# Token-permuted column blocks, and the first z cast, turned and scored block by block, in an attention and MoE kernel

## The chip, the cores and the metric

The kernel runs on one core of one Trainium2 chip. The metric is device microseconds of one execution; "before" takes 1245.67 us (median of 5 runs, 1244.64 to 1246.48). A ratio between two kernels is the mean time of one kernel's fast runs over the mean of the other's fast runs of the same rounds, so it is not quite the ratio of the quoted medians. Names: TensorE is PE in the profile, its weight loads PEld, VectorE is DVE, ScalarE is ACT, GpSimd is POOL, SyncE is SP. A "q" behind a name (ACTq, SPq) is the engine's own queue at work on instructions such as the issue of a DMA.

## The reference

```python
# u, v: (8, 3008, 256), z: (8, 3008, 64), w_in: (256, 2048), w_out: (2048, 256)
scores = (1 / S) * z @ z.T                      # per batch, S = 3008
attn   = maximum(scores, 0) ** 2
x      = u * (attn @ v)                         # gated attention
h      = x.reshape(24064, 256) @ w_in
out    = (h * cos(h)) @ w_out
```

## The kernel before

A batch has 3008 rows: 6 column blocks of 512 (the last has 448), each 4 tiles of 128. For column block c and row block R, TensorE makes four score matmuls, ScalarE and VectorE apply relu and square, and TensorE multiplies with v into two accumulators. The MoE part of earlier tokens is woven in between. Score squares of later blocks (tt) come from DMA transposes of earlier ones. In batch 0 there is nothing earlier to weave in, so its first blocks wait for the loads. The parts that matter here:

```python
def rows(src, b, g):                     # 8 tiles of 128 rows: row j*128 + p on partition p
    r0 = g * G * P
    n = min(G, (S - r0) // P)
    full = src[b, r0:r0 + n * P, :].rearrange("(j p) d -> p j d", p=P)
    rest = src[b, r0 + n * P:S, :] if n < G else None
    return n, full, rest

def hold(dma):                           # a load waits until TensorE has come this far
    after(dma.ins, gate[0] if gate else before[-1], SYNC)
...
def first_z_load(g):                     # 3 groups: 8 loads in all, on SP's and ACT's queues
    ...
    nc.sync.dma_start(zf[:, 0:n // 2, :], full[:, 0:n // 2, :])
    nc.scalar.dma_start(zf[:, n // 2:n, :], full[:, n // 2:n, :])
    if rest is not None:
        nc.scalar.dma_start(zf[0:JLAST, n, :], rest)
        nc.sync.dma_start(zf[JLAST:P, n, :], rest)

def first_z_turn(g):                     # cast on VectorE, 8 transposes on TensorE, copy out
    nc.vector.tensor_copy(zst[:, j0 + 1:j0 + 1 + G, :], zfs[g])
    ...
    (nc.scalar.copy if g < 2 else nc.vector.tensor_copy)(zT[0][:, ...], tp[:, ...])   # shortened
...
# the order of work: an event's first number is its place in time; one column block is 8 long
scores.append((c * U + 4 * i / 3 - 3.1, [(b, c, R, 0), (b, c, R, 1)]))
at((-30, -2.5, 0.8)[g], 0, lambda g=g: first_z_turn(g))
first = [load_v(0, 0), load_u(0, 0), load_v(0, 1), load_v(0, 2), load_u(0, 1)]        # shortened
at(t + c * U + (1 if b or c not in (1, 2) else -3 * c), 0, lambda b=b, c=c: turn_u(b, c))
...
# a store: 256 rows, one DMA on ScalarE's queue
nc.scalar.dma_start(out[r0:r0 + 256, :].rearrange("(ts p) d -> p ts d", p=P), obs[m][:, 0:2, :])  # shortened
```

In PSUM the kernel keeps six rotating score banks and two accumulators.

Of the kernel before, what the change touches and what calls it, by code (L numbers as in the profile page):

```python
# [9 lines left out]
FP16 = mybir.dt.float16  # L10
FP32 = mybir.dt.float32
# [3 lines left out]
def kernel(  # L15
# [44 lines left out]
    ust = [kpool.tile([P, NDH, K, P], FP16, name=f"ust{i}") for i in range(2)]  # L60
# [32 lines left out]
    def rows(src, b, g):  # L93

        r0 = g * G * P
        n = min(G, (S - r0) // P)
        full = src[b, r0:r0 + n * P, :].rearrange("(j p) d -> p j d", p=P)
        rest = src[b, r0 + n * P:S, :] if n < G else None
        return n, full, rest

    def load_z(b):
        for g in range(NG):
            n, full, rest = rows(z, b, g)
            j0 = g * G + 1
            load(zst[:, j0:j0 + n, :], full)
            if rest is not None:
                for p0 in (0, JLAST):
                    load(zst[p0:p0 + JLAST, j0 + n, :], rest)
# [8 lines left out]
    def load_v(b, g):  # L117
        t = vs(b, g)
        n, full, rest = rows(v, b, g)
        load(t[:, 0:n, :], full)  # L120
        if rest is not None:
            for p0 in (0, JLAST):
                load(t[p0:p0 + JLAST, n, :], rest)
# [12 lines left out]
    def load_u(b, c):  # L136
        r0 = c * CW
        n = min(K, (S - r0) // P)
        st = ust[c % 2]
        for dh in range(NDH):  # L140
            ds = slice(dh * P, (dh + 1) * P)
            load(
                st[:, dh, 0:n, :],
                u[b, r0:r0 + n * P, ds].rearrange("(j p) d -> p j d", p=P))
            if n < K:
                load(st[0:JLAST, dh, n, :], u[b, r0 + n * P:S, ds])

    def turn_u(b, c):
        ut = utpool.tile([P, NDH, CW], FP16, name="ut")
        hold(nc.sync.dma_start_transpose(  # L150
            ut.rearrange("p h (j w) -> p (h j) w", w=P),
            ust[c % 2].rearrange("p h j w -> p (h j w)")))
        uts[(b, c)] = ut
# [17 lines left out]
    def first_z_load(g):  # L171
        zfs[g] = xpool.tile([P, NDH, TW], FP16, name="x")
        zf = zfs[g].rearrange("p h w -> p (h w)").bitcast(FP32).rearrange(
            "p (j d) -> p j d", d=dqk)
        zfs[g] = zf
        n, full, rest = rows(z, 0, g)
        nc.sync.dma_start(zf[:, 0:n // 2, :], full[:, 0:n // 2, :])
        nc.scalar.dma_start(zf[:, n // 2:n, :], full[:, n // 2:n, :])
        if rest is not None:
            nc.scalar.dma_start(zf[0:JLAST, n, :], rest)  # L180
            nc.sync.dma_start(zf[JLAST:P, n, :], rest)

    def first_z_turn(g):
        j0 = g * G
        last = g == NG - 1
        nc.vector.tensor_copy(zst[:, j0 + 1:j0 + 1 + G, :], zfs[g])  # L186
        for k, n in ((0, G), (G, 1))[0:1 + last]:
            tp = ps_w.tile([P, CW], FP32, name="w").bitcast(FP16).rearrange(
                "p (j w) -> p j w", w=P)
            for i in range(n):  # L190
                chain(nc.tensor.transpose(  # L191
                    tp[:, i, :],
                    zst[:, j0 + k + i:j0 + k + i + 2, :].rearrange("p j d -> p (j d)"),
                    ident))
            if g < 2:
                nc.scalar.copy(zT[0][:, j0 + k:j0 + k + n, :], tp[:, 0:n, :])  # L196
            else:
                nc.vector.tensor_copy(zT[0][:, j0 + k:j0 + k + n, :], tp[:, 0:n, :])
# [12 lines left out]
    def s_matmuls(b, c, R, p):  # L211
# [5 lines left out]
        for k in ((0, 1), (3, 2) if diagonal else (2, 3))[p]:  # L217
            s0 = k if diagonal else 0
            lo = 1 if k in ((1, 2) if diagonal else (1, 3)) else 0
            h = slice(lo * dqk, (lo + 1) * dqk)  # L220
# [69 lines left out]
    def av_chunks(b, c, sizes):  # L290
# [26 lines left out]
        def finish():  # L317
# [4 lines left out]
            while o < w:  # L322
                m, at = (t0 + o) // TW, (t0 + o) % TW
                n = min(w - o, TW - at)
                if m not in xs:
                    xs[m] = xpool.tile([P, NDH, TW], FP16, name="x")
                parts.append((xs[m][:, :, at:at + n], o, n))
                o += n
            for nh in range(NDH):
                for x, o, n in parts:  # L330
                    nc.vector.tensor_tensor(  # L331
                        x[:, nh, :], acc[nh][:, o:o + n], ut[:, nh, o:o + n], ALU.mult)
# [24 lines left out]
    def y_quantum(m, ts, f4):  # L357
# [6 lines left out]
        if f4 == NFT // FG - 1:  # L364
# [5 lines left out]
            i0 = i if m == NT - 1 else 0  # L370
            if i or m == NT - 1:
                r0 = m * TW + (ts - i + i0) * P
                nc.scalar.dma_start(
                    out[r0:r0 + (i + 1 - i0) * P, :].rearrange("(ts p) d -> p ts d", p=P),
                    obs[m][:, i0:i + 1, :])
# [17 lines left out]
    for b in range(B):  # L393
# [6 lines left out]
        for c in range(NC):  # L400
            if direct(b, c, c):
                for i in range(NC):
                    R = (c + i) % NC
                    scores.append((c * U + 4 * i / 3 - 3.1, [(b, c, R, 0), (b, c, R, 1)]))
# [32 lines left out]
    for b in range(B):  # L437
        t = b * span
        if b == 0:
            for g in range(NG):  # L440
                at(-100 + g, 0, lambda g=g: first_z_load(g))
                at((-30, -2.5, 0.8)[g], 0, lambda g=g: first_z_turn(g))
# [70 lines left out]
```

## Time and profile before

| | before |
|---|---|
| median | 1245.67 us |
| span of the profiled run | 1244.6 us |
| TensorE busy | 1234.4 us, 99% |
| first scores / first value matmul | 7.3 / 11.7 us |
| stall at 40 us | 2.63 us |
| stores | 96 |

The head of the page of before gives the span, and busy time, share of the span and instruction count of each engine:

```profile
span 1244.6 us, 20404 instructions
...
PE 1234.4 (99%) x7533; PEld 680.0 (55%) x7533; DVE 782.0 (63%) x1389; ACT 844.7 (68%) x1609; POOL 145.8 (12%) x201
```

The table by stretches of before: per stretch its length, then the busy time of PE, PEld, DVE, ACT and POOL with instruction counts, the granted clock, the DMA share and GB/s.

```profile
0.00:16.00 16.00, 12.96 (x65) 4.97 (x65) 10.26 (x22) 9.15 (x16) 7.72 (x15) 1.00 1.18 162
16.00:40.00 24.00, 24.00 (x126) 8.33 (x124) 21.27 (x34) 15.72 (x30) 4.29 (x6) 1.00 1.34 148
40.00:43.00 3.00, 0.37 (x5) 0.18 (x2) 0.83 (x2) 1.57 (x3) 0.36 (x1) 1.00 1.22 212
...
50.00:64.00 14.00, 12.67 (x61) 4.90 (x58) 10.97 (x18) 12.28 (x24) 6.14 (x8) 1.00 1.61 151
...
80.00:1240.00 1160.00, 1160.00 (x7151) 649.95 (x7150) 722.10 (x1287) 791.39 (x1511) 123.91 (x167) 1.00 0.71 114
```

From 80 to 1240 us TensorE never stands still, so a change can gain only before and after that. The timeline of before (start, duration, engine, line, what, count; in brackets the idle time before it and who ended it) shows the opening and the stall:

```profile
4.33 0.78 DVE L186 CAST zst<-x 128x512 f16<-128x512 f32 x1 [2.93 <-DMA x<-in_z_dram]
...
6.24 1.01 ACT L196 COPY zT_63<-w 128x1024 f16<-128x1024 f16 x1 [3.46 <-PE w L191]
...
7.30 1.03 PE L223 MATMUL w<-zT_63 64*128 64x512 f16 x4 [1.10 <-ACT zT_63 L196]
...
11.70 1.47 PE L310 MATMUL acc<-a,v_65 128*128 128x512 f16 x6
...
42.17 1.29 DVE L331 TENSOR_TENSOR x<-acc,ut 128x512 f16<-128x512 f32 x2 [2.46 <-DMA ut<-ust_62]
...
42.91 1.46 PE L310 MATMUL acc<-a,v_66 128*128 128x512 f16 x6 [2.63 <-DVE x L331]
```

and the chain of work that ended last (start, duration, what) leads the stall back to a DMA transpose of u:

```profile
31.03 11.05 DMA ut<-ust_62
```

### The profile page before, as it was taken

What the parts mean: (1) busy time and instruction counts of PE and PEld (TensorE: products, weight loads), DVE (VectorE), ACT (ScalarE), POOL (GpSimd) and SP (SyncE); (2) the same over time, 40 slices, a digit from 0 to 9 for tenths busy, and PEclk for the clock granted to TensorE, in tenths of its full rate; (3) what the DMA queues carried; (4) which work ended last, traced back from release to release, by engine and by line L of the source; (5) the groups of instructions that cost most, each with busy time, mean ns of one, the idle gap of its engine ahead of it and who ended that gap; (6) DMA issues with size and microseconds to landing.
All of it is one profiled execution on the core that took longest, in us unless ns stands there. A gap on an engine that the chain in (4) does not pass through costs nothing.

```text
span 1244.6 us, 20404 instructions
## 1 busy us (share of the span) xinstructions
PE 1234.4 (99%) x7533; PEld 680.0 (55%) x7533; DVE 782.0 (63%) x1389; ACT 844.7 (68%) x1609; POOL 145.8 (12%) x201
## 2 busy tenths in 40 slices
PE   9899999999999999999999999999999999999998
PEld 3355555555555555555555555555555555555556
DVE  7766666666666666656666566665666656666555
ACT  6666676666676766667766667766667766667646
POOL 3210101001010010100101011011010111100000
PEclk9999999999999999999999999999999999999999
DMA  9997958679576795757958569685695957957311
GB/s 162 152 174 129 141 91 119 114 122 142 99 117 111 117 144 106 115 111 110 149 101 121 107 109 150 101 129 99 109 158 92 129 101 112 152 101 108 72 33 45
DMA packets 484212, 144.85 MB, mean 116 GB/s; under 512 B 432400, under 2 KB 484112, under 8 KB 484112
## 3 DMA queue, kind: packets, MB, share of 16 engines
q1 hardware_dynamic: 356448, 88.73, 43.1%
q0 software_dynamic: 100400, 29.77, 24.7%
q10 hardware_dynamic: 27264, 25.06, 6.3%
q8 instruction: 59, 0.97, 0.3%
q14 instruction: 41, 0.34, 0.1%
HBM read 60.29 MB, written 24.64 MB: 68 GB/s over the span
## 4 chain that ended last, share of the span: by engine, by line
PE 97%; DMA 2%; DVE 0%; ACT 0%; issue 0%; DVEq 0%; ACTq 0%
PE acc L310 37%; PE w L361 26%; PE w L344 26%; PE w L223 6%; DMA tt<-a 1%; DMA ut<-ust_62 1%; PE acc L285 1%; DMA x<-in_z_dram 0%; DVE g L351 0%; PE w L191 0%; DVE x L331 0%; ACT zT_63 L196 0%; ACT rt L256 0%; DVE a L258 0%; DVE zst L186 0%
## 5 line engine op out<-in xcount | busy, mean ns | idle before, releaser
L361 PE MATMUL w<-w_out_71,g 128*128 128x256 f16 x3008 | 448.6, 273 | 0.0
L344 PE MATMUL w<-x,w_in_70 128*128 128x512 f16 x1504 | 445.6, 379 | 0.8 <-DVE g L351 0.8
L361 PEld LDWEIGHTS <-g 128*128 128x128 f16 x3008 | 294.2, 98 | 191.6 <-issue 1.4
L256 ACT ACTIVATE rt<-w 128x512 f16<-128x512 f32 x489 | 253.1, 613 | 121.2 <-PE w L223 121.2
L258 DVE TENSOR_TENSOR a<-rt 128x1024 f16<-128x1024 f16 x254 | 173.8, 691 | 180.8 <-ACT rt L256 178.3
L344 PEld LDWEIGHTS <-w_in_70 128*128 128x128 f16 x1504 | 147.0, 98 | 59.2 <-issue 3.9
L90 POOL DMA_DIRECT2D ust_62<-in_u_dram x64 | 44.7, 704 | 385.8 <-PE acc L310 355.9
L240 ACT ACTIVATE rt<-w 128x512 f16<-128x512 f32 (+3 forms) x176 | 62.8, 449 | 39.7 <-PE w L223 39.7
L331 DVE TENSOR_TENSOR x<-acc,ut 128x64 f16<-128x64 f32 (+7 forms) x178 | 69.6, 431 | 29.1 <-PE acc L310 26.6
L310 PE MATMUL acc<-a,v_65 128*128 128x512 f16 x336 | 85.8, 380 | 0.0
L310 PEld LDWEIGHTS <-v_66 128*128 128x128 f16 x552 | 51.9, 98 | 61.8 <-issue 14.1
L310 PEld LDWEIGHTS <-v_65 128*128 128x128 f16 x552 | 51.6, 98 | 60.0 <-issue 13.1
L310 PEld LDWEIGHTS <-v_67 128*128 128x128 f16 x552 | 51.9, 98 | 58.7 <-issue 11.1
L310 PEld LDWEIGHTS <-v_68 128*128 128x128 f16 x552 | 51.9, 98 | 57.7 <-issue 10.9
L310 PE MATMUL acc<-a,v_66 128*128 128x512 f16 x312 | 79.4, 379 | 2.6 <-DVE x L331 2.6
L310 PE MATMUL acc<-a,v_68 128*128 128x512 f16 x312 | 79.2, 379 | 0.0
L310 PE MATMUL acc<-a,v_67 128*128 128x512 f16 x312 | 79.1, 379 | 0.0
L368 ACT ACTIVATE ob<-w 128x256 f32<-128x256 f32 x188 | 73.0, 388 | 5.3 <-PE w L361 5.3
L241 DVE TENSOR_TENSOR a<-rt 128x512 f16<-128x512 f16 (+3 forms) x176 | 47.3, 321 | 44.0 <-ACT rt L240 44.0
L90 POOL DMA_DIRECT2D ust_61<-in_u_dram x48 | 36.5, 766 | 224.4 <-PE acc L310 206.7
L310 PE MATMUL acc<-tt,v_68 128*128 128x512 f16 (+1 forms) x240 | 62.2, 371 | 0.0
L310 PE MATMUL acc<-tt,v_67 128*128 128x512 f16 (+1 forms) x240 | 62.1, 371 | 0.0
(1546 smaller groups left out, 1399.8 us busy)
## 6 DMA issues: line engine op xcount, KB each, us to landing
out_dram<-ob ACTq DMA_DIRECT2D x92, 256.0 KB, 2.3
ust_61<-in_u_dram POOLq DMA_DIRECT2D x48, 128.0 KB, 4.0
ust_62<-in_u_dram POOLq DMA_DIRECT2D x32, 128.0 KB, 4.4
a<-a SPq DMA_TRANSPOSE x132, 3.0
v_65<-in_v_dram POOLq DMA_DIRECT2D x4, 512.0 KB, 6.1
v_66<-in_v_dram POOLq DMA_DIRECT2D x4, 512.0 KB, 6.6
v_68<-in_v_dram POOLq DMA_DIRECT2D x4, 512.0 KB, 6.2
v_67<-in_v_dram POOLq DMA_DIRECT2D x4, 512.0 KB, 6.2
```

The source lines that it names most:

```text
L90: hold(nc.gpsimd.dma_start(dst, src))
L223: chain(nc.tensor.matmul(sp[:, s0 * P:], zt[h, R * K + k + 1 - lo, :], zt[h, j0 + s0:j0 + K, :].rearrange("p j w -> p (j w)"), start=True, ...
L240: nc.scalar.activation(rt[:, i, k * P:], banks[k][:, k * P:], AF.Relu)
L241: nc.vector.tensor_tensor(t[:, k, k:, :].rearrange("p s w -> p (s w)"), rt[:, i, k * P:], rt[:, i, k * P:], ALU.mult)
L256: nc.scalar.activation(rt[:, i, :], banks[k], AF.Relu)
L258: nc.vector.tensor_tensor(t.rearrange("p s k w -> p k s w")[:, 2 * p:2 * p + 2], rv, rv, ALU.mult)
L285: chain(nc.tensor.matmul(accs[(b, c)][nh], vs(b, NG - 1)[h, G - 1, nh * P:(nh + 1) * P], a[h], start=False, stop=False))
L310: chain(nc.tensor.matmul(acc[nh][:, 0:wn], vs(b, j // G)[:, j % G, nh * P:(nh + 1) * P], a, start=(n == 0), stop=(n == NJ - 2)))
L331: nc.vector.tensor_tensor(x[:, nh, :], acc[nh][:, o:o + n], ut[:, nh, o:o + n], ALU.mult)
L344: chain(nc.tensor.matmul(hp, w_in16[:, k, ft * P:(ft + 1) * P], x[:, k, :], start=(k == 0), stop=(k == NDH - 1)))
L361: chain(nc.tensor.matmul(ys[m][:, 0:D], gs[(m, f4)][:, ft % FG, ts * P:(ts + 1) * P], w_out16[:, ft, :], start=(ft == 0), stop=(ft == NFT ...
L368: nc.scalar.activation(obs[m][:, i, :], ys[m][:, 0:D], AF.Copy, bias=0.0, scale=inv_s2)
```

## The change

Rows of a column block are dealt out so that partition p holds rows 4p to 4p + 3 of the block. Each partition's piece of z, v, u and out is then contiguous in DRAM: 1 KB instead of 256 B for z, 4 KB instead of 1 KB for v, 4 KB instead of 512 B for u. The first z is loaded, cast, turned and scored per column block instead of per group of 8 tiles, so that the first scores need only a sixth of z. u of block 1 is loaded and turned earlier. The price: output tiles of 512 tokens and column blocks are shifted against each other by 64 rows per batch, so a store often has to be cut into 64-partition pieces. Cut to its core:

```diff
-        full = src[b, r0:r0 + n * P, :].rearrange("(j p) d -> p j d", p=P)
+        full = src[b, r0:r0 + n * P, :].rearrange("(p k) d -> p k d", k=n)
 ...
+    def first_z_load(c):                 # 6 blocks x 2 halves + 2 for the rest: 14 loads
 ...
+        for p0, eng in ((0, nc.sync), (JLAST, nc.scalar)):
+            h = slice(p0, p0 + JLAST)
+            eng.dma_start(zfs[c // 2][h, k0:k0 + n, :], full[h])
+            if rest is not None:
+                eng.dma_start(zfs[c // 2][h, k0 + n, :], rest)
 ...
-                    scores.append((c * U + 4 * i / 3 - 3.1, [(b, c, R, 0), (b, c, R, 1)]))
+                    t = c * U + 4 * i / 3 - 3.1 if c else (-3.1, -1.8, 0.6, 1.9, 3.2, 4.4)[i]
+                    scores.append((t, [(b, c, R, 0), (b, c, R, 1)]))
 ...
-                at((-30, -2.5, 0.8)[g], 0, lambda g=g: first_z_turn(g))
+                at((-30, -2.9, 0.55, 1.85, 3.15, 4.35)[c], 0, lambda c=c: first_z_turn(c))
-            first = [load_v(0, 0), load_u(0, 0), load_v(0, 1), load_v(0, 2), load_u(0, 1)]
+            first = [load_v(0, 0), load_u(0, 0), load_v(0, 1), load_u(0, 1), load_v(0, 2)]
-            at(t + c * U + (1 if b or c not in (1, 2) else -3 * c), 0, ... turn_u(b, c))
+            at(t + c * U + 1 if b or c > 2 else (1, 1.8, 5)[c], 0, ... turn_u(b, c))
 ...
-                nc.scalar.dma_start(out[...], obs[m][:, i0:i + 1, :])       # 96 stores
+                store(m, ts, ...)        # 1 to 4 pieces of 64 or 128 partitions, 184 in all
 ...
-        for i in range(8): warming matmul; the loads of v and u are let go after the fifth
+        warm(4); the loads of v and u are let go; warm(2); 2 more behind the first transposes
```

More of the change, by code (lines that the diff above doesn't have):

```diff
@@ L59 @@
     zst = kpool.tile([P, NJ + 2, dqk], FP16, name="zst")
-    ust = [kpool.tile([P, NDH, K, P], FP16, name=f"ust{i}") for i in range(2)]
+    ust = [kpool.tile([P, K, D], FP16, name=f"ust{i}") for i in range(2)]
     zT = [kpool.tile([P, NJ + 1, P], FP16, name=f"zT{i}") for i in range(2)]
@@ L90, in load, with rows, load_rows @@
         hold(nc.gpsimd.dma_start(dst, src))
-    def rows(src, b, g):
-        r0 = g * G * P
-        n = min(G, (S - r0) // P)
-        full = src[b, r0:r0 + n * P, :].rearrange("(j p) d -> p j d", p=P)
-        rest = src[b, r0 + n * P:S, :] if n < G else None
-        return n, full, rest
-    def load_z(b):
-        for g in range(NG):
-            n, full, rest = rows(z, b, g)
-            j0 = g * G + 1
-            load(zst[:, j0:j0 + n, :], full)
-            if rest is not None:
-                for p0 in (0, JLAST):
-                    load(zst[p0:p0 + JLAST, j0 + n, :], rest)
+    def rows(src, b, c):
+        r0 = c * CW
+        n = min(K, (S - r0) // P)
+        full = src[b, r0:r0 + n * P, :].rearrange("(p k) d -> p k d", k=n)
+        rest = src[b, r0 + n * P:S, :] if n < K else None
+        return n, full, rest
+    def load_rows(t, j0, src, b, c, lanes):
+        n, full, rest = rows(src, b, c)
+        load(t[:, j0:j0 + n, :], full)
+        if rest is not None:
+            for p0 in lanes:
+                load(t[p0:p0 + JLAST, j0 + n, :], rest)
+    def load_z(b):
+        for c in range(NC):
+            load_rows(zst, c * K + 1, z, b, c, (0, JLAST))
     def turn_z(b):
@@ L117, in load_v @@
     def load_v(b, g):
-        t = vs(b, g)
-        n, full, rest = rows(v, b, g)
-        load(t[:, 0:n, :], full)
-        if rest is not None:
-            for p0 in (0, JLAST):
-                load(t[p0:p0 + JLAST, n, :], rest)
+        for i in range(G // K):
+            load_rows(vs(b, g), i * K, v, b, g * G // K + i, (0, JLAST))
     def load_w_in(q):
@@ L136, in load_u @@
     def load_u(b, c):
-        r0 = c * CW
-        n = min(K, (S - r0) // P)
-        st = ust[c % 2]
-        for dh in range(NDH):
-            ds = slice(dh * P, (dh + 1) * P)
-            load(
-                st[:, dh, 0:n, :],
-                u[b, r0:r0 + n * P, ds].rearrange("(j p) d -> p j d", p=P))
-            if n < K:
-                load(st[0:JLAST, dh, n, :], u[b, r0 + n * P:S, ds])
+        load_rows(ust[c % 2], 0, u, b, c, (0,))
     def turn_u(b, c):
-        ut = utpool.tile([P, NDH, CW], FP16, name="ut")
+        ut = utpool.tile([P, K, NDH, P], FP16, name="ut")
         hold(nc.sync.dma_start_transpose(
-            ut.rearrange("p h (j w) -> p (h j) w", w=P),
-            ust[c % 2].rearrange("p h j w -> p (h j w)")))
+            ut.rearrange("p k h w -> p (k h) w"), ust[c % 2].rearrange("p k d -> p (k d)")))
         uts[(b, c)] = ut
@@ L169 @@
     zfs = {}
-    def first_z_load(g):
-        zfs[g] = xpool.tile([P, NDH, TW], FP16, name="x")
-        zf = zfs[g].rearrange("p h w -> p (h w)").bitcast(FP32).rearrange(
-            "p (j d) -> p j d", d=dqk)
-        zfs[g] = zf
-        n, full, rest = rows(z, 0, g)
-        nc.sync.dma_start(zf[:, 0:n // 2, :], full[:, 0:n // 2, :])
-        nc.scalar.dma_start(zf[:, n // 2:n, :], full[:, n // 2:n, :])
-        if rest is not None:
-            nc.scalar.dma_start(zf[0:JLAST, n, :], rest)
-            nc.sync.dma_start(zf[JLAST:P, n, :], rest)
@@ L183, in first_z_turn @@
-    def first_z_turn(g):
-        j0 = g * G
-        last = g == NG - 1
-        nc.vector.tensor_copy(zst[:, j0 + 1:j0 + 1 + G, :], zfs[g])
-        for k, n in ((0, G), (G, 1))[0:1 + last]:
-            tp = ps_w.tile([P, CW], FP32, name="w").bitcast(FP16).rearrange(
-                "p (j w) -> p j w", w=P)
-            for i in range(n):
-                chain(nc.tensor.transpose(
-                    tp[:, i, :],
-                    zst[:, j0 + k + i:j0 + k + i + 2, :].rearrange("p j d -> p (j d)"),
-                    ident))
-            if g < 2:
-                nc.scalar.copy(zT[0][:, j0 + k:j0 + k + n, :], tp[:, 0:n, :])
-            else:
-                nc.vector.tensor_copy(zT[0][:, j0 + k:j0 + k + n, :], tp[:, 0:n, :])
+    def first_z_load(c):
+        if c % 2 == 0:
+            zfs[c // 2] = xpool.tile([P, NDH, TW], FP16, name="x").rearrange(
+                "p h w -> p (h w)").bitcast(FP32).rearrange("p (j d) -> p j d", d=dqk)
+        k0 = c % 2 * K
+        n, full, rest = rows(z, 0, c)
+        for p0, eng in ((0, nc.sync), (JLAST, nc.scalar)):
+            h = slice(p0, p0 + JLAST)
+            eng.dma_start(zfs[c // 2][h, k0:k0 + n, :], full[h])
+            if rest is not None:
+                eng.dma_start(zfs[c // 2][h, k0 + n, :], rest)
@@ new lines, in first_z_turn @@
+    def first_z_turn(c):
+        j0 = c * K
+        nc.vector.tensor_copy(
+            zst[:, j0 + 1:j0 + 1 + K, :], zfs[c // 2][:, c % 2 * K:c % 2 * K + K, :])
+        n = K + (c == NC - 1)
+        tp = ps_w.tile([P, CW], FP32, name="w").bitcast(FP16).rearrange(
+            "p (j w) -> p j w", w=P)
+        for i in range(n):
+            chain(nc.tensor.transpose(
+                tp[:, i, :], zst[:, j0 + i:j0 + i + 2, :].rearrange("p j d -> p (j d)"),
+                ident))
+        if c < NC - 2:
+            nc.scalar.copy(zT[0][:, j0:j0 + n, :], tp[:, 0:n, :])
+        else:
+            nc.vector.tensor_copy(zT[0][:, j0:j0 + n, :], tp[:, 0:n, :])
@@ L219, in s_matmuls @@
             lo = 1 if k in ((1, 2) if diagonal else (1, 3)) else 0
+            if b == c == R == 0:
+                lo = 1
             h = slice(lo * dqk, (lo + 1) * dqk)
@@ L324, in finish @@
                 n = min(w - o, TW - at)
+                k0, w0 = divmod(o, P)
+                if w0:
+                    n = min(n, P - w0)
+                elif n > P:
+                    n -= n % P
                 if m not in xs:
                     xs[m] = xpool.tile([P, NDH, TW], FP16, name="x")
-                parts.append((xs[m][:, :, at:at + n], o, n))
+                parts.append((
+                    xs[m][:, :, at:at + n], o, n,
+                    ut[:, k0, :, w0:w0 + n] if n < P else ut[:, k0:k0 + n // P, :, :]))
                 o += n
             for nh in range(NDH):
-                for x, o, n in parts:
-                    nc.vector.tensor_tensor(
-                        x[:, nh, :], acc[nh][:, o:o + n], ut[:, nh, o:o + n], ALU.mult)
+                for x, o, n, us in parts:
+                    if n < P:
+                        xo, ao, uo = x[:, nh, :], acc[nh][:, o:o + n], us[:, nh, :]
+                    else:
+                        xo, ao = (a.rearrange("p (k w) -> p k w", w=P)
+                                  for a in (x[:, nh, :], acc[nh][:, o:o + n]))
+                        uo = us[:, :, nh, :]
+                    nc.vector.tensor_tensor(xo, ao, uo, ALU.mult)
         ends = [min(sum(sizes[:i]), NJ - 1) for i in range(len(sizes) + 1)]
@@ L369, in y_quantum, with place, store @@
                 obs[m][:, i, :], ys[m][:, 0:D], AF.Copy, bias=0.0, scale=inv_s2)
-            i0 = i if m == NT - 1 else 0
             if i or m == NT - 1:
-                r0 = m * TW + (ts - i + i0) * P
-                nc.scalar.dma_start(
-                    out[r0:r0 + (i + 1 - i0) * P, :].rearrange("(ts p) d -> p ts d", p=P),
-                    obs[m][:, i0:i + 1, :])
+                store(m, ts, range(0 if m < NT - 1 else i, i + 1))
+    HB = JLAST
+    def place(pos):
+        b, r = divmod(pos, S)
+        c, o = divmod(r, CW)
+        k, p0 = divmod(o, P)
+        n = min(K, (S - c * CW) // P)
+        t0 = b * S + c * CW
+        return (t0 + p0 * n + k, n) if k < n else (t0 + n * P + p0, 1)
+    def store(m, ts, which):
+        todo = []
+        for h in range(P // HB):
+            for i in which:
+                pos = m * TW + (ts - ts % 2 + i) * P + h * HB
+                tok, step = place(pos)
+                if todo and step > 1 and todo[-1][0] == h * HB and todo[-1][5] == step \
+                        and tok == todo[-1][4] + 1 and tok % S % CW % step:
+                    p0, np_, i0, ni, t0, _ = todo.pop()
+                    todo.append((p0, np_, i0, ni + 1, t0, step))
+                else:
+                    todo.append((h * HB, HB, i, 1, tok, step))
+        merged = []
+        for x in todo:
+            p0, np_, i0, ni, t0, step = x
+            for y in merged:
+                if y[0] + y[1] == p0 and y[2:4] == x[2:4] and y[5] == step \
+                        and t0 == y[4] + y[1] * step:
+                    merged.remove(y)
+                    x = (y[0], y[1] + np_, i0, ni, y[4], step)
+                    break
+            merged.append(x)
+        for p0, np_, i0, ni, t0, step in merged:
+            b, r = divmod(t0, S)
+            k = (r % CW) % step
+            if step > 1:
+                dst = out[t0 - k:t0 - k + np_ * step, :].rearrange(
+                    "(p k) d -> p k d", k=step)[:, k:k + ni, :]
+            else:
+                dst = out[t0:t0 + np_, :].rearrange("(p k) d -> p k d", k=1)
+            nc.scalar.dma_start(dst, obs[m][p0:p0 + np_, i0:i0 + ni, :])
     events = []
@@ L439 @@
         if b == 0:
-            for g in range(NG):
-                at(-100 + g, 0, lambda g=g: first_z_load(g))
-                at((-30, -2.5, 0.8)[g], 0, lambda g=g: first_z_turn(g))
+            for c in range(NC):
+                at(-100 + c, 0, lambda c=c: first_z_load(c))
+                at((-30, -2.9, 0.55, 1.85, 3.15, 4.35)[c], 0, lambda c=c: first_z_turn(c))
             first = [lambda: load_v(0, 0), lambda: load_u(0, 0), lambda: load_v(0, 1),
-                     lambda: load_v(0, 2), lambda: load_u(0, 1)]
+                     lambda: load_u(0, 1), lambda: load_v(0, 2)]
             for i, f in enumerate(first):
@@ L459, with warm @@
         for c in range(NC):
-            at(t + c * U + (1 if b or c not in (1, 2) else -3 * c), 0, lambda b=b, c=c: turn_u(b, c))
+            at(t + c * U + 1 if b or c > 2 else (1, 1.8, 5)[c], 0, lambda b=b, c=c: turn_u(b, c))
     dummy = kpool.tile([P, 1], FP32, name="dummy")
+    zeros = []
+    def warm(n):
+        wp = ps_w.tile([P, CW], FP32, name="w")
+        for i in range(n):
+            chain(nc.tensor.matmul(
+                wp, zeros[0][:, 0, 0:P], zeros[0][:, 0, :], start=True, stop=True))
     def prepare():
@@ L467, in prepare @@
         nc.vector.memset(zero[:, 0, :], 0.0)
-        wp = ps_w.tile([P, CW], FP32, name="w")
-        for i in range(8):
-            chain(nc.tensor.matmul(
-                wp, zero[:, 0, 0:P], zero[:, 0, :], start=True, stop=True))
-            if i == 4:
-                gate.append(before[-1])
+        zeros.append(zero)
+        warm(4)
+        gate.append(before[-1])
+        warm(2)
         make_identity(nc, ident)
@@ L476, in prepare @@
         nc.vector.memset(zst[:, NJ + 1, :], 0.0)
-        nc.vector.memset(ust[1][:, :, K - 1, :], 0.0)
+        nc.vector.memset(ust[1][:, K - 1, :], 0.0)
     at(-101, 0, prepare)
+    at(-29, 0, lambda: warm(2))
     events.sort(key=lambda e: e[:3])
```

## The prediction

> **What bounds it now.** The page's busy table gives TensorE 1234.4 us of a 1244.6 us span (99%), granted clock 1.0. Its matmuls are back to back: in the chain of work that ended last, twelve 512-column value matmuls take 2.59 us, 216 ns each[...]. The table by stretches shows no TensorE idle from 80 to 1240 us. VectorE (63%), ScalarE (68%) and DMA are not limits there. TensorE's order outside the opening and its instruction count (7533) are unchanged. So only the first 80 us and the last 4 us can move.
>
> **Lost in the opening now** (timeline): first z lands at 4.3 us, first scores 7.3, first value matmul 11.7, then TensorE is dense. At 40.3 it stops 2.63 us: the output multiply waits for the turned u of block 1, a DMA transpose issued only at 31.0, behind three score transposes, landing 11.05 us later. From 50 to 64 us it idles another 1.3 us (squares wait for score transposes).
>
> **Removed.**
> 1. Block 1's u is now turned before the score transposes: that stall goes, 2.6 us.
> 2. u's pieces grow from 512 B to 4 KB, z's from 256 B to 1 KB, v's from 1 KB to 4 KB. I expect the software queue's 100,400 packets to fall to about a quarter. After the opening loads are off the path: worth 0 to 0.8 us through quicker score transposes.
> 3. Smaller first z pieces: first scores at about 5.3, first value matmul at about 9.5 us.
>
> **Added.** Blocks 2 to 5 of z are now turned directly before the scores that need them, so TensorE waits each time for the copy out of PSUM. Costed from the trace: transpose latency 0.2 + copy of 512 columns 0.55 + semaphores = about 0.85 us with ScalarE (1024 columns take 1.01), 1.2 us where VectorE copies behind its squares; about 4 us in all, plus 0.9 before the second scores. Before, only 1.1 us was so waited. Following the three engines' order through the opening with the trace's durations gives before's end of block 0 right (25.2 us) and puts after's at 28 to 29: the opening loses about 3 us, which eats item 1.
>
> **Moved, off the path.** Stores go from 96 to 184 (0.35 us of ScalarE's queue each, +31 us); some 46 more short output multiplies (0.22 us, +10 us of VectorE). In steady state the six score banks should cover this. At the end two half stores instead of one: +0.3 us.
>
> **Sum.** -2.6 (u) -0.5 (score transposes) -2 (early start) +5 (waits for copies) -1 (earlier waits that go) +0.3 (tail) = about -1: 1245 us. Range 1241.5 to 1248. Chances: faster by over 2% 0.01, within 2% 0.985, slower 0.005.
>
> **What would show it.** Right: no TensorE idle before block 2's value matmuls behind an output multiply; four or five idles of 0.5 to 1.5 us before score matmuls released by zT copies between 7 and 22 us; end of block 0 at 27 to 29 us; no idle from 80 us on; lower DMA share without effect. Wrong: end of block 0 at 23 to 25 us (then about 1241), or idle in the steady stretch behind ScalarE's stores.
>
> **What would make it wrong.** The zT waits may be hidden (up to -4 us). The clock may stay low longer, as TensorE idles more early (+1 us). Four stores in a row (1.4 us) before a score visit could hold up squares in odd batches (up to +5 us in all). Score transposes may queue behind u of block 1 (+1 us).

## More of the kernel before

In both packed traces the DMAs that SyncE and ScalarE issue use eight completion semaphores between them. The 8 z loads of before use eight different ones, and none of them waits.

## The result, and the profile after

The changed kernel takes 1258.11 us (median of 5 runs, 1256.34 to 1259.92) against 1245.67; ratio 1.0101, 95% interval 1.0087 to 1.0116. It is slower by 1%, within the class of 2%, but outside the predicted range of 1241.5 to 1248. The page's head and the table by stretches of the changed kernel:

```profile
span 1258.1 us, 20585 instructions
...
PE 1240.7 (99%) x7533; PEld 680.2 (54%) x7533; DVE 788.0 (63%) x1474; ACT 844.4 (67%) x1611; POOL 100.5 (8%) x190
```

```profile
0.00:16.00 16.00, 8.83 (x27) 2.89 (x28) 5.19 (x16) 5.53 (x9) 6.14 (x16) 1.00 0.87 171
16.00:40.00 24.00, 21.12 (x96) 7.52 (x95) 15.81 (x27) 11.75 (x23) 2.60 (x4) 1.00 0.78 110
40.00:43.00 3.00, 3.00 (x18) 0.84 (x16) 2.95 (x6) 2.27 (x5) 0.39 (x2) 1.00 1.27 177
...
50.00:64.00 14.00, 13.92 (x74) 5.11 (x71) 12.53 (x21) 9.91 (x19) 5.19 (x10) 1.00 1.18 178
...
80.00:1250.00 1170.00, 1167.42 (x7185) 651.89 (x7182) 732.14 (x1379) 795.84 (x1521) 82.60 (x155) 1.00 0.65 113
```

In the first 40 us TensorE starts 123 matmuls where before it started 191. The instruction counts say more here than the busy times: 21.12 of 24 us busy looks nearly full, but 96 matmuls in that time are a quarter fewer than 126.

**The ledger.** Both traces hold 7533 matmuls, and outside the opening in the same order. I numbered them by start and took the difference of the start times of equal numbers. It stays constant for hundreds of matmuls and steps where one kernel waits and the other does not:

| from the start to | step, us | so far |
|---|---|---|
| 31 us: block 0 of batch 0 | +12.78 | +12.78 |
| 55 us: the stall on u is gone | -2.55 | +10.23 |
| 72 us: the waits at 50 to 64 us are gone | -0.95 | +9.28 |
| last matmul: five small steps, four in odd batches, one (0.72) in batch 2 | +3.32 | +12.60 |
| end of span (4.39 us after the last matmul starts, 3.42 before) | +0.97 | +13.57 |

The profiled run is the slowest of the changed kernel's five (1259.92 us), so this sum is above the 12.44 us between the medians.

The opening in the timeline of the changed kernel:

```profile
0.75 3.76 SPq L170 DMA_DIRECT2D x<-in_z_dram  x6
...
2.91 2.77 ACTq L170 DMA_DIRECT2D x<-in_z_dram  x3
...
3.44 1.21 POOL L90 DMA_DIRECT2D v_65<-in_v_dram  x2 [2.13 <-PE w L513]
...
5.71 0.78 ACTq L172 DMA_DIRECT2D x<-in_z_dram  x1
...
6.54 0.58 ACT L186 COPY zT_63<-w 128x512 f16<-128x512 f16 x1 [3.68 <-issue]
...
7.18 1.88 PE L215 MATMUL w<-zT_63 64*128 64x512 f16 x4 [1.93 <-ACT zT_63 L186]
...
10.43 0.29 DVE L176 CAST zst<-x 128x256 f16<-128x256 f32 x1 [4.60 <-DMA x<-in_z_dram]
...
12.70 0.29 DVE L176 CAST zst<-x 128x256 f16<-128x256 f32 x1 [1.98 <-DMA x<-in_z_dram]
12.91 0.68 DVE L246 TENSOR_SCALAR rt<-w 128x512 f16<-128x512 f32 x1
13.65 0.61 PE L215 MATMUL w<-zT_63 64*128 64x512 f16 x2 [2.76 <-DVE rt L246]
...
14.45 1.01 PE L302 MATMUL acc<-a,v_65 128*128 128x512 f16 x2 [0.19 <-DVE a L250]
...
19.78 2.74 PE L302 MATMUL acc<-a,v_65 128*128 128x512 f16 x6
...
28.80 1.47 PE L302 MATMUL acc<-a,v_66 128*128 128x512 f16 x6
```

Three things stand here. ScalarE is at the issue of its last z loads until 6.5 us; the transposes it should copy out were done at 4.4 us. VectorE must do six casts before its first square, and the last casts wait for z until 10.4 and 12.7 us. And six value matmuls take 2.74 us at 19.8 us, 1.47 us at 28.8 us: until 27.6 us TensorE runs at half its clock (neighbouring value matmuls start 0.426 us apart before that, 0.216 us after it). The chain of work that ended last says what the 12.7 us come from:

```profile
2.00 2.50 DMA x<-in_z_dram
...
4.51 0.49 ACTq L170
...
5.05 0.63 ACTq L170
...
5.71 6.87 DMA x<-in_z_dram
...
12.70 0.29 DVE zst L176
```

The z load that ScalarE issues at 4.51 had to wait until an earlier one had landed, at 4.49. ScalarE's queue is idle for 0.98 us before it (inside the merged line of 2.91), and this is the only wait of that length on either queue: SyncE issues its seven loads one right behind the other, until 5.14 us. Five z loads are issued after v's first load (3.44). The last of them, issued at 5.71, needed 6.87 us to land, the other four 5.16 to 6.71; of the nine issued before v, eight needed 2.14 to 2.52 us and the last (3.27) 4.05.

A warning on the clock column: the table by stretches prints 1.00 in all of these stretches. The packed trace holds records of the granted clock with their times. The first one says 1.0 from 27.59 us on here, from 10.45 us on in before, and the second, after the last work, 0.5. What lies ahead of the first record is not low in the views; it has to be read from the spacing of the matmuls.

In the steady stretch the waits of TensorE from 80 us on are:

```profile
PE w L348 <- ACT rt L232: 2.0, 2, 1.6
PE w L348 <- ACT rt L248: 0.4, 1, 0.4
```

### The profile page after: what moved, and what is told of

It reads as the page before. It is cut to its first block, busy times and chain, and to the rows that moved or that the text cites. A ratio compares the mean times of both kernels' runs of the same rounds, so it can differ in the third digit from the quotient of the medians.

```text
span 1258.1 us, 20585 instructions
## 1 busy us (share of the span) xinstructions
PE 1240.7 (99%) x7533; PEld 680.2 (54%) x7533; DVE 788.0 (63%) x1474; ACT 844.4 (67%) x1611; POOL 100.5 (8%) x190
## 3 DMA queue, kind: packets, MB, share of 16 engines
q0 software_dynamic: 26112, 29.77, 17.0%
## 4 chain that ended last, share of the span: by engine, by line
PE 95%; ACT 2%; DMA 1%; issue 1%; DVE 0%; ACTq 0%; SPq 0%; DVEq 0%
PE acc L302 37%; PE w L365 26%; PE w L348 26%; PE w L215 6%; ACT rt L248 1%; PE acc L277 1%; DMA x<-in_z_dram 1%; ACTq L419 0%; DVE a L250 0%; ACT rt L232 0%; PE w L182 0%; ACT ob L372 0%; ACT zT_63 L186 0%; SPq L170 0%; ACTq L170 0%
## 5 line engine op out<-in xcount | busy, mean ns | idle before, releaser
L336 DVE TENSOR_TENSOR x<-acc,ut 128x64 f16<-128x64 f32 (+4 forms) x260 | 75.4, 342 | 27.0 <-PE acc L302 23.6
L302 PE MATMUL acc<-a,v_65 128*128 128x512 f16 x336 | 89.4, 391 | 0.6 <-DVE a L250 0.6
L302 PE MATMUL acc<-a,v_66 128*128 128x512 f16 x312 | 80.1, 382 | 0.1
L302 PE MATMUL acc<-a,v_68 128*128 128x512 f16 x312 | 79.2, 380 | 0.0
L302 PE MATMUL acc<-a,v_67 128*128 128x512 f16 x312 | 79.1, 380 | 0.0
L302 PE MATMUL acc<-tt,v_68 128*128 128x512 f16 (+1 forms) x240 | 62.3, 371 | 0.0
L302 PE MATMUL acc<-tt,v_67 128*128 128x512 f16 (+1 forms) x240 | 62.1, 371 | 0.0
L302 PE MATMUL acc<-tt,v_66 128*128 128x512 f16 (+1 forms) x240 | 61.9, 371 | 0.0
L215 PE MATMUL w<-zT_63 64*128 64x512 f16 x348 | 49.2, 372 | 8.9 <-ACT zT_63 L186 4.0
```

Source lines behind the costliest of these rows:

```text
L215: chain(nc.tensor.matmul(sp[:, s0 * P:], zt[h, R * K + k + 1 - lo, :], zt[h, j0 + s0:j0 + K, :].rearrange("p j w -> p (j w)"), start=True, ...
L302: chain(nc.tensor.matmul(acc[nh][:, 0:wn], vs(b, j // G)[:, j % G, nh * P:(nh + 1) * P], a, start=(n == 0), stop=(n == NJ - 2)))
L336: nc.vector.tensor_tensor(xo, ao, uo, ALU.mult)
```

## The experiments

The question is where 12.8 us go in block 0, and 3.3 us in the steady stretch. The theories, by the letters that the expectations use:

- **A: z comes late because 14 loads share 8 semaphores.** Issues wait for landings, ScalarE's queue is held and with it the first copy. A1 says that the held issue alone makes the late loads late; A2 says that they are late because v and u have been issued ahead of them. A rival within A is that 14 issues simply take longer than 8, semaphores or not.
- **B, rival: the waits for zT copies** that the prediction had costed, only longer.
- **C, the clock:** TensorE idles so much that it is kept at half its clock. This is a consequence of A or B, but has a size of its own.
- **D, rival: the permuted tokens** make the loads themselves worse.
- **The stores:** twice as many issues on ScalarE's queue hold up relu in odd batches, against the rival that VectorE's extra output multiplies do it.

Eleven runs. The table gives what was read from each profile: from when the clock was full by the trace's records, the end of the last cast of the first z, and, as in the ledger, how far TensorE is behind before's profiled run after block 0, at 100 us, and at the last matmul. For runs with added matmuls the numbering is from the end.

| run | clock full from | last cast ends | block 0 | 100 us | last matmul | median us |
|---|---|---|---|---|---|---|
| before | 10.5 | 7.5 | 0 | 0 | 0 | 1245.67 |
| changed | 27.6 | 13.0 | +12.78 | +9.28 | +12.60 | 1258.11 |
| e1_eight_loads | 4.7 | 6.3 | +1.76 | -1.74 | +0.66 | 1247.38 |
| e11_eight_and_six | 23.2 | 12.7 | +11.03 | +7.53 | +9.34 | 1256.76 |
| e6_v_held | 4.8 to 8.2, 15.0 | 7.9 | +6.57 | +3.07 | +4.47 | 1252.63 |
| e3_keep_warm | 4.8 to 15.1, 21.9 | 12.9 | +10.65 | +7.15 | +9.87 | 1253.15 |
| e7_all_warm | 6.3 | 12.9 | +7.96 | +4.46 | +5.43 | 1252.68 |
| e2_old_stores | 5.6 to 9.0, 22.7 | 13.1 | +11.35 | +7.85 | +7.85 | 1254.21 |
| e4_old_opening | 10.6 | 6.4 | -0.52 | -4.03 | -2.83 | 1244.37 |
| e8_turned_ahead | 13.9 | 6.4 | +2.96 | -0.54 | +1.31 | 1247.64 |
| e5_u_first | 5.9 to 60.6, 67.4 | 7.5 | -0.70 | +1.96 | +2.10 | 1249.05 |
| e9_stores_two_queues | 4.0 | 6.5 | -1.92 | -4.16 | -3.93 | 1243.04 |
| e10_clock_kept | 6.0 | 6.6 | -1.16 | -4.36 | -3.89 | 1243.45 |

The kernel before itself lay between 1242.1 and 1247.7 us in these rounds, so differences under about 2 us are read from the ledger, not from the medians. But the ledger holds one profile of each kernel, and part of it is luck: e4 and e9 have the same opening, yet the clock is full from 10.6 us in one and from 4.0 us in the other, and block 0 differs by 1.4 us. (The expectations of e8 and e9 quote 1.55 us for e1's block 0 and 1.3 us for e4's steady loss; recounted, they are 1.76 and 1.20.)

### e1_eight_loads: the changed kernel with 8 z loads instead of 14

```diff
-        for p0, eng in ((0, nc.sync), (JLAST, nc.scalar)):
-            h = slice(p0, p0 + JLAST)
-            eng.dma_start(zfs[c // 2][h, k0:k0 + n, :], full[h])
-            if rest is not None:
-                eng.dma_start(zfs[c // 2][h, k0 + n, :], rest)
+        eng = (nc.sync, nc.scalar)[c % 2]
+        eng.dma_start(zfs[c // 2][:, k0:k0 + n, :], full)
+        if rest is not None:
+            nc.scalar.dma_start(zfs[c // 2][0:JLAST, k0 + n, :], rest)
+            nc.sync.dma_start(zfs[c // 2][JLAST:P, k0 + n, :], rest)
```

> The changed kernel with the first z loaded in 8 pieces (one of 128 partitions per block, two for the rest) instead of 14, all else as changed. Theory A (the 14 loads outnumber the 8 completion semaphores, so ScalarE's queue holds up its first copy, the last z pieces are issued after v and land at 12.6 us, and the long wait leaves TensorE's clock low): ScalarE's first zT copy starts at about 4.5 us instead of 6.5, the sixth cast ends by 8 us instead of 13.0, TensorE is at full rate by about 15 us instead of 28, block 0 ends 8 to 10 us earlier; about 1249 us. Rival B (what my prediction named: the transposes placed directly before their scores): the waits for zT copies stay and the gain is under 3 us, about 1256 us.

Measured: 1247.38 us, ratio to before 1.0018 (0.9995 to 1.0042). The timeline of this run:

```profile
4.46 0.58 ACT L186 COPY zT<-w 128x512 f16<-128x512 f16 x1 [1.77 <-PE w L182]
...
6.26 0.67 DVE L246 TENSOR_SCALAR rt<-w 128x512 f16<-128x512 f32 x1
...
8.48 1.72 PE L302 MATMUL acc<-a,v 128*128 128x512 f16 x6 [0.73 <-DMA v<-in_v_dram]
```

The first copy starts at 4.46, the first square's relu at 6.26, the first value matmul at 8.48 us, as theory A said; the gain is 11.0 us in block 0, more than the 8 to 10 expected. The waits for copies that the prediction named are still there, and are still about 4 us in all:

```profile
PE w L215 <- ACT zT L186: 2.0, 3, 0.7
PE w L215 <- DVE zT L188: 2.0, 2, 1.0
```

So those waits are real, but with the early start they leave block 0 only 1.76 us behind before. Rival B falls as the explanation of 12.8.

### e11_eight_and_six: e1 with six small loads added

```diff
         eng.dma_start(zfs[c // 2][:, k0:k0 + n, :], full)
+        (nc.scalar, nc.sync)[c % 2].dma_start(zscr[:, c, :], z[0, c * CW:c * CW + JLAST, :])
```

> The run with 8 whole z loads (1247.4 us, last cast ended at 6.3 us, first zT copy on ScalarE at 4.5 us), with six small loads of 16 KB into an unused tile put between them, so that 14 loads share the 8 completion semaphores again; the pieces that matter keep their shape. If the number of loads over the number of semaphores is the cause (theory A1): ScalarE's queue waits again between its later loads, its first zT copy starts at 5.5 us or later, the last cast ends after 9 us, block 0 ends 4 us or more later than with 8 loads, total 1251 or more. If the shape of the pieces (64 partitions on each of two queues) was the cause: the copy and the casts stay within 1 us of the run with 8 loads, total within 1.5 us of 1247.4.

Measured: 1256.76 us, ratio 1.0100 (1.0079 to 1.0122). The timeline of this run:

```profile
5.85 0.58 ACT L188 COPY zT<-w 128x512 f16<-128x512 f16 x1 [3.01 <-PE w L515]
...
12.36 0.29 DVE L178 CAST zst<-x 128x256 f16<-128x256 f32 x1 [6.36 <-DMA x<-in_z_dram]
...
13.31 0.61 PE L217 MATMUL w<-zT 64*128 64x512 f16 x2 [3.11 <-DVE rt L248]
```

Six loads of 16 KB, which nobody reads, bring back 9.3 of the 11.0 us. The number of loads is the cause, and the shape of z's pieces is not the main part of it. This run doesn't tell the two ways apart in which the number can act, waits for semaphores and plain issue time, and no other run does. The traces give the larger part to issue time: ScalarE's last z issue ends at 6.50 us in the changed kernel and at 2.72 in e1. Of these 3.78 us, 2.72 are the issues themselves (seven in 4.53 us against four in 1.81), and 0.98 is the wait for a semaphore. SyncE's queue has no gap over 0.08 us between its seven issues. In e11 ScalarE's queue stands still for 0.38, 0.92 and 0.28 us between its z issues, about 1.5 us beyond the usual gaps of 0.04 us. In e1 all z loads have been issued by 2.72 us, before v's first load at 3.43.

### e6_v_held: the changed kernel, v and u held until the first scores

```diff
             for i, f in enumerate(first):
-                at(-80 + i, 0, f)
-            at(-70, 0, gate.clear)
+                at(-3.05 + i * 0.001, 0, f)
 ...
         warm(4)
-        gate.append(before[-1])
         warm(2)
```

> The changed kernel (still 14 z loads) with the first loads of v and u held until the first scores' last matmul[...]. If the last z pieces are late because v's larger pieces sit in front of them (theory A2), they land by about 8 us instead of 12.6, though they are still issued late; v then comes later, at about 13 to 14 us, and sets the first value matmul; total 1 to 3 us shorter than the changed kernel, 1255 to 1257. If they are late only because their issue is held by the semaphores (A1), the last z lands no earlier than 12 us and the total is 1259 or more.

Measured: 1252.63 us, ratio 1.0067 (1.0040 to 1.0095). The timeline of this run:

```profile
5.50 0.61 ACTq L172 DMA_DIRECT2D x<-in_z_dram  x1
...
7.63 0.29 DVE L176 CAST zst<-x 128x256 f16<-128x256 f32 x1 [0.91 <-DMA x<-in_z_dram]
```

The last z is cast at 7.63 us, though ScalarE's queue still issues its last z load only at 5.50 us. So A2: the late pieces are late because v and u were issued ahead of them. With v and u held, the last z load is cast 2.13 us after its issue began (5.50 to 7.63); behind v, in the changed kernel, it needed 6.87 us to land, against 2.14 to 2.52 us for eight of the nine z loads ahead of v. By what mechanism v's loads delay z's was not shown. The gain was larger than I expected (5.5 instead of 1 to 3 us), since the first value matmul came at 12.1 us, not at 13 to 14, and the clock was full from 15.0 us.

### e3_keep_warm and e7_all_warm: the changed kernel with filling matmuls

```diff
+    FILL = {(0, 0, 0, 0): 4, (0, 0, 1, 0): 2, (0, 0, 1, 1): 8}     # e3: 14 in all
+    # e7: {(0, 0, 0, 0): 6, (0, 0, 1, 0): 4, (0, 0, 1, 1): 17}, and 3 before the first value matmul
+    def fill(n):
+        for i in range(n):
+            chain(nc.tensor.matmul(accs[(0, 0)][0], zeros[...], zeros[...], start=True, stop=True))
 ...
+        if (b, c, R, p) in FILL:
+            fill(FILL[(b, c, R, p)])
```

> The changed kernel with 14 matmuls on zeros put into TensorE's early waits (4 before the first scores, 2 and 8 around the second), into the accumulator that the first real matmul clears. All loads and all waits stay. Theory C (half of the opening's loss is the low clock after the 2.8 us wait): the first six value matmuls per chunk take about 1.4 us instead of 2.7 from 14.5 us on, block 0 ends 4 to 6 us earlier, about 1253 us. If the low clock is only a companion of the waits and VectorE is what TensorE waits for, the end of block 0 moves under 1.5 us and the total is 1257 or more.

Measured for e3: 1253.15 us (1252.16 to 1257.34), ratio 1.0063. The profiled run is the slowest of the four: its clock was full at 4.8 us, fell to half at 15.1, after a gap of 2.0 us that the fillers did not cover, and rose at 21.9. So its block 0 moved only 2.1 us; the other three runs were 3 to 5 us shorter. For that the second run was made, with the gaps filled:

> The changed kernel with enough matmuls on zeros to fill all of TensorE's early waits (6 before the first scores, 4 and 17 around the second, 3 before the first value matmul); all 14 z loads and their lateness stay. e3 with 14 fillers still let the clock fall at 15.1 us and rise again at 21.9 us. If the loss of 12.8 us in block 0 is about 6 of late z, about 5 of low clock and 1.5 to 2 of waits for copies: the clock is full from about 5 us on without a break, the first value matmul still comes at about 14.5 us, block 0 ends 7 to 8.5 us later than in before, and all runs lie near 1252.5 us, within 1.5 us of each other. If the clock matters less, block 0 ends 10 us or more later and the total is above 1255.

Measured for e7: 1252.68 us, four runs within 0.5 us; ratio 1.0053 (1.0038 to 1.0068). (Fillers may only write an accumulator that holds nothing yet, so they could not be put everywhere.) The timeline of e7: the first value matmul comes at 14.79 us, as late as in the changed kernel, but at full rate:

```profile
14.79 1.62 PE L316 MATMUL acc<-a,v 128*128 128x512 f16 x6
```

Block 0 is 7.96 us behind before instead of 12.78: the low clock costs 4.8 us in these two profiles.

### e4_old_opening: permuted tokens with the opening of before

```diff
-    first_z_load(c), first_z_turn(c) and score times of the change
+    first_z_load(g), first_z_turn(g) and score times of before; a group's z as two loads of 4 rows each
```

> The changed kernel (permuted tokens, half stores, u first) with the opening of before: z cast and turned in groups of 8 tiles, two ahead, 8 z loads of 1 KB pieces, 8 warming matmuls, scores at the old times. All theories that put the loss into the opening: TensorE's matmuls stand within 1 us of before's at 25 us (+12.8 in the changed kernel), the gains of u (-2.5) and of 50 to 64 us (-0.9) stay, and the losses in the steady stretch (+3.3) and at the end (+0.9) stay: 1246 to 1247 us. If permuted loads themselves slow the opening (rival D: v's 4 KB pieces crowd out z), the first value matmul comes over 2 us later than 11.7 and the total is above 1248.

Measured: 1244.37 us (four runs, 1244.31 to 1244.92), ratio 0.9996 (0.9973 to 1.0019). Block 0 is 0.52 us ahead of before; u's stall and the waits behind it are gone (-3.5 us), the steady steps are +1.2 us here instead of the expected 3.3, so the total is below the expected 1246 to 1247. Rival D falls: the permuted loads do not harm the opening. All of the changed kernel's loss in the opening comes from how it loads, turns and schedules the first z, with the warming matmuls around it, which this run puts back too.

### e8_turned_ahead: e1 with each block turned one step earlier

```diff
-                at((-30, -2.9, 0.55, 1.85, 3.15, 4.35)[c], 0, lambda c=c: first_z_turn(c))
+                at((-30, -3.0, -1.75, 0.65, 1.95, 3.25)[c], 4, lambda c=c: first_z_turn(c))
```

> The kernel of the run with 8 z loads, with each block of z turned one step ahead, behind the scores of the block before it, instead of directly before its own scores. If the 4 us of waits for zT copies that were left there are real losses: most of them go, block 0 ends 1.5 to 3 us earlier than there (it was 1.55 us later than before's), total about 1245. If they only stand in for VectorE's pace, the waits turn into others and the total stays within 1 us of 1247.4.

Measured: 1247.64 us (1245.61 to 1249.01), ratio 1.0011: no gain, against the expectation. ScalarE's waits fell from 2.0 to 0.7 us, but VectorE's two copies are still waited for, 2.0 us. And in this profiled run the clock was full only from 13.9 us, in e1's from 4.7 us. Which of the two ate the gain I cannot say; this run is inconclusive.

### e2_old_stores: the changed kernel with 96 stores

```diff
-                store(m, ts, range(0 if m < NT - 1 else i, i + 1))
+                nc.scalar.dma_start(out[r0:...].rearrange("(ts p) d -> p ts d", p=P), obs[m][:, i0:i + 1, :])
```

> The changed kernel with the stores of before (one per two groups of rows, 96 in all), which put the permuted rows in the wrong places: the result is wrong on purpose. If the doubled stores on ScalarE's queue cause TensorE's idle in the steady stretch (3.3 us in the profiled run of the changed kernel) and the longer end (0.9 us): no TensorE idle between 85 us and the end, the last matmul as far behind before's as the ones at 100 us, total 3 to 4.5 us less than the changed kernel, 1254 to 1255. If the extra short output multiplies on VectorE cause it: the idles stay and the total is 1257 or more.

Measured: 1254.21 us (1253.89 to 1254.59), result wrong as intended. From 85 us on the profile lists no wait of TensorE at all; the lag is +7.85 us at 100 us and +7.85 at the last matmul; the span ends 3.52 us after the last matmul starts (4.39 in the changed kernel). The extra output multiplies on VectorE are still in it. So the stores cause the steady loss. Its size varies: in the eight profiles with 184 stores on ScalarE's queue the lag grows by 0.97 us (e7) to 3.32 us (the changed kernel) from 100 us to the last matmul. What happens there, in the changed kernel's timeline:

```profile
607.84 2.60 ACTq L419 DMA_DIRECT2D out_dram<-ob  x2
...
608.37 0.66 PE L215 MATMUL w<-zT_63 64*128 64x512 f16 x6
...
610.48 1.42 ACT L232 ACTIVATE rt<-w 128x512 f16<-128x512 f32 x4 [2.68 <-PE acc L302]
...
611.13 0.59 PE L348 MATMUL w<-x,w_in_70 128*128 128x512 f16 x2 [1.61 <-ACT rt L232]
```

ScalarE is at two store issues for 2.60 us while six filled score banks wait for its relu; TensorE then finds no free bank for 1.61 us. A store in before took 0.34 to 0.45 us to issue, every one of the 96. In the changed kernel the second of two back to back mostly takes 0.61, and a few take 1.1 to 2.1 us. Why those few are so long was not tested.

### e5_u_first: the kernel before with u of block 1 loaded and turned earlier

```diff
-            first = [load_v(0, 0), load_u(0, 0), load_v(0, 1), load_v(0, 2), load_u(0, 1)]
+            first = [load_v(0, 0), load_u(0, 0), load_v(0, 1), load_u(0, 1), load_v(0, 2)]
-            at(t + c * U + (1 if b or c not in (1, 2) else -3 * c), 0, ... turn_u(b, c))
+            at(t + c * U + 1 if b or c > 2 else (1, 1.8, 5)[c], 0, ... turn_u(b, c))
```

> The kernel before with one thing from the change: u of block 1 loaded before the last third of v and turned before the score transposes. If that order alone is what took away the 2.6 us stall at 40 us: the stall is gone, and TensorE is 2.5 to 3.5 us earlier than in before from 65 us on; about 1243 us. If the stall went only because larger pieces of u and v landed sooner: it stays, or moves to another wait, and the total is within 1 us of before.

Measured: 1249.05 us (1246.84 to 1250.38), ratio 1.0022 (1.0005 to 1.0039): slower than before. The stall is gone (TensorE is 3.25 us ahead at 50 us), but at 100 us it is 1.96 us behind. The view of the score transposes' tile tells who waited for those transposes up to 90 us:

```profile
  DVE a L258: 5.2, 3
```

VectorE waited 5.2 us for the transposes to release score tiles (none in the same view of e4 or of the changed kernel), TensorE stood still behind it, and the clock fell to half from 60.6 to 67.4 us, which the table by stretches of this run shows, as it does not lie ahead of the first record:

```profile
48.00:64.00 16.00, 12.82 (x53) 4.68 (x51) 10.85 (x18) 11.72 (x23) 5.49 (x8) 0.89 1.51 207
64.00:80.00 16.00, 16.00 (x79) 7.49 (x78) 9.57 (x18) 9.46 (x18) 0.75 (x1) 0.89 0.79 139
```

With the old, small pieces the order of u alone gains nothing: the stall moves on to the score transposes. In e4, with the same order and permuted loads, both waits are gone. That the larger pieces are what makes the transposes come sooner is the likely reading (DMA share 1.47 there against 1.61 in before from 50 to 64 us), but no run changed the pieces alone.

### e9_stores_two_queues and e10_clock_kept: the best of the pieces

```diff
 # e9: e4 with
-            nc.scalar.dma_start(dst, obs[m][p0:p0 + np_, i0:i0 + ni, :])
+            (nc.scalar, nc.gpsimd)[x % 2].dma_start(dst, obs[m][p0:p0 + np_, i0:i0 + ni, :])
-    opool = pool("o", 2)
+    opool = pool("o", 4)
 # e10: e9 with
+    FILL = {(0, 0, 0, 0): 3}
```

> The kernel with the old opening and the permuted tokens (it measured 1244.4 us), with every second piece of a store issued from GpSimd's queue instead of ScalarE's, and four output buffers instead of two. If ScalarE's queue time for the second pieces causes the steady idle (1.3 us there, 3.3 in the changed kernel) and the longer end: no TensorE idle from 80 us to the last matmul, the end after the last matmul shorter by about 0.5 us, total about 1242.5. If GpSimd's queue holds the stores back behind loads that wait: new waits of ScalarE for output buffers, total above 1244.4.

> As the run with stores from two queues, with three matmuls on zeros in front of the first scores, where TensorE waits 1.1 us. If the moment at which the clock becomes full is set by the first unbroken stretch of work: it comes at 5 to 8 us in each run instead of about 10.5, the runs lie within 1 us of each other, and the total is 0 to 1 us shorter than there, about 1242. If not: no difference, or up to 0.3 us longer by the three matmuls.

Measured for e9: 1243.04 us (1242.35 to 1244.93), ratio to before 0.9986 (0.9965 to 1.0007). Of the steady loss 0.2 us is left (1.2 in e4). The end did not get shorter: 4.66 us after the last matmul starts (4.27 in e4), so that part of the expectation missed. e9 beats the changed kernel by 15 us; against before the interval reaches 1, so a gain there is not shown. Measured for e10: 1243.45 us, one of six runs at 1250.59, ratio 0.9998 (0.9966 to 1.0029): no gain from the three matmuls. Its profiled run was at full clock from 6.0 us, e9's without them from 4.0, so what sets that moment is not shown.

## Why the prediction was wrong

Point by point:

- **What bounds the kernel, and where it can move:** right. TensorE is busy for 1160.00 of the 1160 us from 80 to 1240 us in before; all that changed lies in the opening, in the stores of the steady stretch, and in the tail.
- **"that stall goes, 2.6 us":** right, -2.55 us. The reason given, the order, is not enough by itself (e5).
- **Packets to a quarter, 0 to 0.8 us from quicker transposes:** right; 100,400 became 26,112 on the software queue, and the waits at 50 to 64 us shrank by 0.95 us (that the one brought the other was not shown).
- **Waits for zT copies, "about 4 us in all":** right as a term, 4.0 us in e1. In the changed kernel they are 5.5 us, with the one of 1.93 us that ScalarE's held queue caused.
- **"Smaller first z pieces: first scores at about 5.3, first value matmul at about 9.5 us": this is the step that failed.** They came at 7.2 and 14.45 us. With 8 loads instead of 14 they come at 5.1 and 8.5 us (e1). The prediction counted the size of the pieces and not their number. It says nothing of what 14 issues do to ScalarE's queue, where they hold up the first copy to 6.54 us, nor that five z loads are then issued behind v and land as late as 12.6 us, nor that VectorE does all six casts before its first square.
- **"The clock may stay low longer, as TensorE idles more early (+1 us)":** named, but mis-sized; it is 4.8 us (e7, with the gaps filled, against the changed kernel). The 1 us was the author's estimate, worked out from no number of the trace.
- **"In steady state the six score banks should cover this":** wrong, by 3.3 us in the changed kernel's profiled run and by 1 to 3 us in the others with these stores; it stood in the list of risks, as "up to +5 us", but not in the sum. **"At the end +0.3 us"** was +0.97.

The loss of 12.78 us in block 0 can be split by the runs: 4.8 us low clock (changed against e7), 6.2 us late z and held queue (7.96 in e7 against 1.76 in e1), 1.76 us left. The parts are not independent: the same late z makes the gap of 2.76 us, and with the gaps filled (e7) the clock was full from 6.3 us instead of 27.6.

The clock can be followed in the records, but what makes it rise or fall these runs do not show. The stretches between one record and the next are 3.41 us (e2, e6), 6.83 (e3, e5, e6), 10.24 (e3), 13.65 (e2) and 54.61 (e5), each within 0.05 us of a whole multiple of the shortest. In the last 3.41 us before 27.59 us, from which the changed kernel's clock is full, TensorE has no wait; in each of the two stretches of that length ahead of it, from 17.35 and from 20.76 us, it has one of 0.68 us for a zT copy. But short waits alone do not decide it: e7, whose clock was full beforehand, kept it through waits of 0.7 to 1.0 us for copies. Nor does the longest wait: in before the clock stayed full through the stall of 2.63 us at 40 us, in e3 it fell at 15.1 us after waits of 2.0 and 0.8 us, and in e5 it fell at 60.6 us though the longest wait in the 3.41 us before was 1.2 us. In size it is small, 4.8 us of 1258, but more than the change gained (2.55 us by u and 0.95 us behind it).

## What to carry to other kernels

Count the loads at the start, not only their bytes: here 14 loads of z instead of 8, in smaller pieces, put block 0 back by 11.0 us (changed against e1), and six added loads of 16 KB alone by 9.3 us (e11 against e1). Each took 0.5 to 0.8 us to issue in the changed kernel, one issue waited 0.98 us for an earlier load's landing besides, and both held ScalarE's first copy up to 6.54 us (4.46 in e1) and let v's first loads go ahead of five of z's. A loss of a few microseconds at the start can come with a low clock for longer: TensorE ran at half its clock until 27.6 us in the changed kernel, until 4.7 us in e1. The clock column may not show it (it printed 1.00 in these stretches); compare the spacing of equal matmuls (0.426 against 0.216 us here). When a wait is taken away, ask which one stands behind it: in e5 the stall of 2.6 us went and VectorE then waited 5.2 us for transposes. When stores are split, ask whose queue issues them: the second of two back to back mostly took 0.61 us on ScalarE's queue, against 0.34 to 0.45 us for each store of before.
